# Rotary attention with a SoLU MoE layer on one core: a new order of issue, new second engines and new buffers for the same instructions

## Chip, core and metric

The kernel runs on one core of a Trainium2 chip. The core has five engines that run side by side, each with a queue of its own in program order: PE multiplies matrices, DVE and ACT work on tiles elementwise, POOL (GpSimd) does the same more slowly, and SP only issues DMA transfers. The metric is the time of one execution on the device in microseconds (us), the median of several runs; lower is better.

## The reference

Attention with rotary position embedding on 4 batches of 8 heads (576 positions, 64 values each), then a layer on the 2304 tokens of 512 values that come out of it:

```python
q_rot, k_rot = (rotate(q), rotate(k))
scores = scale * np.matmul(q_rot, k_rot.transpose(0, 1, 3, 2))
scores = scores - np.max(scores, axis=-1, keepdims=True)
attn = np.exp(scores)
attn = attn / (np.sum(attn, axis=-1, keepdims=True) + 1e-09)
return np.matmul(attn, v).astype(np.float32)
...
h = x @ w_in
h_max = np.max(h, axis=-1, keepdims=True)
e = np.exp(h - h_max)
sm = e / (np.sum(e, axis=-1, keepdims=True) + 1e-09)
solu = h * sm
mu = np.mean(solu, axis=-1, keepdims=True)
var = np.mean((solu - mu) ** 2, axis=-1, keepdims=True)
ln = (solu - mu) / np.sqrt(var + 1e-06) * g_ln
return (ln @ w_out).astype(np.float32)
```

All is float32. `w_in` is 512x1024 and `w_out` 1024x512; both arrive as float64 bit patterns.

## The kernel before

**Tiles and stages.** Two heads make a pair, P0 to P15, four pairs to a batch; `attention(P)` (line 389) does one. A pair has nine score tiles of 128 rows by 576 columns: four row blocks times two heads, and a packed one for the 64 rows left over of each head. Each goes through the same steps: scores on PE (L421, L450 to L453, L444), the row maximum on DVE (L401, L464), the exponential on ACT (L403, L467), a transpose, and the product with V on PE (`av`, L556), which is done in two ranges of query columns. "A15.1" is the second range of the last pair. DVE scales that product into `xT` (L561). The transpose is done on PE with a copy out of PSUM (`tr`, L481, copies by L324 on ACT or L326 on DVE), or, from pair 4 on for 7 or 8 of the 8 full tiles, by a round trip of the exponentials through DRAM (`escr`) and a 32x32 block transpose on DVE (L502).

**Rope.** `rope` (line 357) turns q and k of a pair ahead of its attention: two products with the tables of cosine and sine and a sum, each 128x576, by `tt` (line 351, all at L355). From pair 4 on, q and k are split in a rounded high part (a cast, L324 or L326) and a low part (a subtraction, L355), and each score is the sum of three products.

**The layer.** When the four pairs of a batch are done, their tokens go in 18 tiles of 128 through `front` (line 606: x split in high and low part, 24 matmuls L626, maximum L633, exponential L635, product L637, a DRAM round trip) and `back` (line 662: block transposes L681, high and low part L686 and L691, 24 matmuls L699, scaling L702 and L704, the store). `weights` (line 748) turns the float64 weights into high and low parts beside the first pairs' attention: for each of 16 pieces a load, a step on ACT (L777), four on DVE (L779, L781, L783, L785), a cast and a subtraction. `norm` (line 565) turns the sums of exponentials into reciprocals (L570, L571) and spreads them by DRAM (`rscr`, `Rb`).

**What sets the order.** All these functions only write down steps: `add` (line 203) keeps for each of 2365 steps its engine, its function and what it reads and writes. The steps are then issued in the order of the list `ORDER` (line 31), so each engine's queue is that list, cut down to its own steps; the semaphores that steps of different engines need follow from what they read and write. A step with `alt=` has a second engine that can do it as well (products, sums and subtractions by `tt`: DVE or POOL; casts and copies: ACT or DVE), and it goes there where its number stands in `FLIP` (line 161). A step of a rope runs on POOL unless flipped, a product of the prologue on DVE. `BUFS` (line 168) has a digit for each of 401 uses of a buffer, out of three score buffers of two PSUM banks ("D", `pd`), two of one bank ("G", `pg`) and three in SBUF ("B", `tb`). All three tables were written by a planner outside this file. The loop that issues:

```python
    for us, b in zip(pl.uses, BUFS):
        us[2] = int(b)
    engines = {"act": nc.scalar, "dve": nc.vector, "pool": nc.gpsimd}
    with tc.manual_schedule():
        for i in ORDER:
            if i in pl.alts:
                a = pl.alts[i]
                pl.ops[i][3](engines[a[2] if i in FLIP else a[0]])
            else:
                pl.ops[i][3]()
```

**The first steps.** `prologue` (line 709) loads the tables (steps 5 and 6), k (8 for the first half of its features, 9 and 10 for the second in two pieces) and q (7 for 192 columns, 11 for the rest), and ropes pair 0 in pieces: q's first 192 columns by steps 16, 17 and 18, its other 384 by 24, 25 and 26, k by 19 (576 columns), 20 and 21 (288), 22 and 23 (288). The first scores need 18, 21 and 23.

Of the kernel before, what the change touches and what calls it, by code (L numbers as in the profile page):

```python
# [31 lines left out]
    2, 3, 4, 5, 8, 6, 10, 7, 9, 11, 27, 35, 19, 12, 22, 23, 17, 20, 21, 16, 91, 18, 43, 25, 102, 24, 26, 28,  # L32
    105, 92, 99, 103, 106, 13, 29, 36, 111, 30, 31, 104, 37, 109, 114, 107, 93, 110, 112, 115, 32, 113, 135,
    38, 108, 51, 39, 33, 116, 122, 123, 138, 97, 124, 117, 136, 125, 139, 118, 126, 40, 120, 119, 144, 137,
    94, 59, 121, 96, 95, 44, 155, 128, 41, 145, 127, 142, 147, 129, 45, 42, 148, 100, 130, 156, 14, 143,
    131, 98, 132, 157, 1, 133, 146, 151, 134, 101, 46, 186, 152, 163, 164, 47, 52, 0, 165, 153, 177, 187,
    166, 167, 154, 140, 189, 188, 158, 48, 141, 195, 159, 178, 168, 190, 169, 53, 179, 160, 67, 149, 196,
    161, 162, 170, 193, 198, 197, 181, 184, 150, 219, 194, 34, 199, 180, 191, 206, 171, 182, 207, 192, 222,
    172, 68, 220, 173, 54, 221, 174, 55, 175, 223, 69, 202, 183, 70, 60, 185, 176, 228, 203, 56, 49, 50,
    208, 200, 229, 209, 210, 239, 201, 231, 230, 71, 224, 232, 72, 226, 225, 61, 212, 270, 73, 62, 211, 63,  # L40
    227, 75, 74, 437, 204, 240, 235, 205, 271, 241, 213, 265, 273, 214, 236, 215, 272, 509, 264, 216, 217,
    274, 275, 266, 279, 276, 64, 269, 57, 218, 83, 76, 58, 244, 237, 282, 245, 246, 238, 277, 280, 283, 233,
    261, 281, 303, 247, 278, 248, 77, 234, 78, 249, 350, 306, 250, 251, 284, 304, 307, 242, 262, 312, 243,
    351, 305, 253, 252, 263, 84, 288, 254, 323, 285, 290, 268, 79, 65, 80, 289, 66, 255, 313, 256, 473, 257,
    291, 314, 315, 258, 352, 324, 316, 259, 15, 292, 260, 293, 325, 85, 294, 317, 86, 267, 438, 308, 87,
    357, 362, 309, 331, 358, 345, 81, 295, 296, 318, 82, 332, 286, 363, 328, 287, 330, 329, 88, 364, 346,
    326, 365, 333, 353, 446, 371, 361, 327, 334, 439, 335, 366, 347, 310, 372, 321, 311, 374, 297, 440, 375,
    360, 298, 441, 299, 373, 354, 300, 322, 301, 447, 382, 442, 395, 474, 448, 455, 666, 302, 337, 380, 398,
    336, 369, 381, 396, 319, 370, 449, 397, 367, 450, 399, 404, 451, 368, 660, 464, 89, 415, 661, 320, 90,
    348, 383, 405, 384, 376, 385, 475, 386, 378, 377, 349, 338, 406, 416, 339, 407, 379, 340, 341, 662, 408,  # L50
    409, 476, 465, 675, 477, 342, 417, 388, 343, 387, 665, 355, 456, 677, 359, 478, 410, 667, 344, 479, 482,
    389, 678, 390, 452, 391, 680, 679, 356, 676, 392, 466, 393, 681, 423, 467, 400, 457, 685, 688, 394, 401,
    682, 424, 761, 512, 425, 413, 513, 689, 426, 427, 414, 411, 691, 690, 402, 468, 714, 692, 469, 480, 696,
    765, 518, 403, 481, 686, 470, 519, 715, 717, 520, 683, 693, 483, 458, 521, 459, 412, 418, 718, 701, 514,
    702, 460, 716, 722, 515, 484, 697, 668, 485, 725, 429, 486, 419, 663, 487, 703, 516, 704, 664, 471, 726,
    705, 420, 517, 672, 694, 422, 728, 727, 430, 431, 684, 766, 723, 531, 432, 491, 421, 433, 488, 730, 687,
    434, 489, 532, 719, 435, 729, 522, 737, 674, 767, 707, 695, 523, 537, 428, 706, 538, 490, 738, 461, 699,
    524, 533, 768, 669, 700, 539, 492, 731, 724, 735, 770, 772, 534, 443, 527, 720, 493, 535, 739, 494, 495,
    540, 444, 740, 496, 445, 536, 736, 698, 500, 777, 497, 525, 498, 436, 708, 472, 778, 550, 709, 732, 710,
    779, 551, 711, 453, 712, 782, 746, 526, 776, 741, 499, 713, 556, 747, 721, 742, 557, 528, 501, 673, 748,  # L60
    552, 749, 502, 670, 750, 733, 503, 553, 783, 504, 734, 743, 462, 505, 554, 463, 780, 506, 588, 555, 752,
    541, 781, 754, 751, 454, 755, 507, 785, 744, 745, 542, 756, 753, 508, 867, 757, 758, 543, 558, 774, 784,
    559, 545, 544, 760, 510, 592, 786, 569, 762, 560, 593, 594, 775, 589, 606, 788, 511, 590, 759, 561, 591,
    791, 789, 570, 792, 595, 562, 790, 596, 796, 671, 529, 793, 814, 801, 530, 563, 802, 769, 866, 803, 597,
    804, 817, 603, 805, 598, 815, 818, 797, 599, 607, 771, 816, 825, 763, 819, 610, 608, 794, 764, 838, 826,
    624, 600, 822, 828, 827, 609, 601, 839, 829, 602, 868, 820, 862, 878, 833, 604, 869, 798, 799, 611, 605,
    613, 830, 840, 612, 614, 795, 564, 615, 546, 881, 823, 547, 616, 841, 861, 879, 617, 882, 628, 618, 800,
    863, 886, 787, 571, 806, 834, 836, 619, 565, 876, 821, 548, 837, 807, 864, 575, 831, 873, 847, 865, 880,
    824, 620, 883, 889, 625, 877, 549, 566, 621, 887, 808, 874, 848, 890, 809, 810, 892, 891, 811, 622, 893,
    576, 894, 962, 835, 629, 849, 915, 626, 850, 832, 851, 627, 812, 884, 577, 902, 623, 870, 578, 813, 903,  # L70
    916, 904, 572, 918, 917, 961, 842, 888, 573, 905, 920, 919, 854, 900, 773, 574, 871, 843, 897, 901, 872,
    963, 923, 926, 579, 895, 853, 844, 630, 927, 906, 580, 855, 852, 845, 856, 929, 928, 967, 857, 885, 898,
    858, 846, 930, 921, 859, 581, 966, 924, 936, 931, 938, 937, 896, 582, 968, 978, 875, 860, 939, 631, 973,
    899, 940, 632, 969, 633, 922, 941, 970, 634, 932, 981, 635, 908, 925, 982, 567, 636, 642, 568, 986, 979,
    989, 947, 980, 637, 990, 639, 983, 638, 933, 907, 971, 991, 909, 640, 964, 910, 994, 992, 1015, 977,
    965, 948, 993, 643, 942, 987, 974, 997, 911, 943, 1016, 912, 984, 644, 1018, 913, 1017, 645, 1000, 914,
    1002, 1001, 1020, 934, 949, 646, 1026, 935, 950, 951, 1003, 1252, 944, 1027, 995, 955, 946, 945, 956,
    1028, 1029, 1253, 957, 998, 988, 1030, 976, 1004, 958, 1019, 1254, 1005, 985, 959, 1006, 1023, 1037,
    1039, 952, 647, 1038, 583, 954, 996, 649, 648, 953, 1021, 1264, 1040, 1034, 584, 999, 1041, 650, 1007,
    1042, 651, 1265, 1008, 1247, 652, 1267, 1266, 1024, 653, 1248, 1031, 1268, 585, 1269, 654, 641, 960,  # L80
    1022, 1249, 1275, 1035, 1009, 1276, 586, 1010, 587, 1048, 1011, 1277, 1278, 1012, 1259, 1013, 1032,
    1025, 1301, 1263, 1280, 1014, 1279, 1270, 1062, 655, 1272, 1063, 657, 656, 1283, 1049, 1288, 1262, 1250,
    1050, 1064, 1051, 1251, 1052, 1068, 1033, 1065, 1069, 1036, 1353, 1043, 1302, 1070, 1281, 1044, 1304,
    1066, 1303, 1352, 658, 1071, 1305, 1271, 1045, 1273, 1255, 1067, 1047, 1256, 1284, 1312, 1081, 1072,
    1309, 1306, 1056, 972, 1315, 1073, 1054, 1057, 1053, 1313, 1348, 1058, 975, 1316, 1046, 1074, 1314,
    1324, 1354, 1289, 1317, 1286, 1325, 1055, 1059, 1082, 1359, 1287, 1060, 1326, 1282, 1310, 1364, 1327,
    1347, 1285, 1307, 1257, 1076, 1087, 1363, 1349, 1365, 1290, 1088, 1291, 1274, 1292, 1328, 1089, 1077,
    1329, 1318, 1367, 1090, 1366, 1075, 1333, 1334, 1322, 1061, 1368, 1083, 1311, 1323, 1375, 1355, 1308,
    1335, 1320, 1336, 1378, 1084, 1337, 1321, 1453, 1362, 1376, 1085, 1379, 1294, 1319, 1293, 1330, 1377,
    1086, 1078, 1357, 1260, 1157, 1401, 1100, 1091, 1338, 1332, 1331, 1101, 1350, 1339, 1295, 1402, 1340,  # L90
    1092, 1296, 1383, 1297, 1404, 1079, 1372, 1341, 1454, 1093, 1405, 1342, 1403, 1343, 1409, 1388, 1258,
# [818 lines left out]
```

## Time and profile before

| what | value |
|---|---|
| three runs, us | 448.65, 453.29, 454.40 |
| median of the runs, us | 453.29 |
| profiled execution, span from its first to its last instruction, us | 452.4 |
| TensorE's granted clock in it | 1.000 |
| instructions in it | 8070 |
| HBM read and written, MB | 70.91 and 37.82 |

The span is the profiled execution's own time as far as it is known: no other time is told for that execution, and what lies around its first and last instruction is in the runs' times alone. The median of the runs is 0.9 us above the span.

A time at an engine's instruction is from its start to its end as the profiler saw it. DVE's and POOL's instructions overlap their neighbours by up to 0.1 us. PE's matmuls are pipelined, so a matmul's record is longer than the time that it adds; the chain that ended last counts only what it adds.

### The profile page before, as it was taken

What the parts mean: (1) busy time and instruction counts of PE and PEld (TensorE: products, weight loads), DVE (VectorE), ACT (ScalarE), POOL (GpSimd) and SP (SyncE); (2) the same over time, 40 slices, a digit from 0 to 9 for tenths busy, and PEclk for the clock granted to TensorE, in tenths of its full rate; (3) what the DMA queues carried; (4) which work ended last, traced back from release to release, by engine and by line L of the source; (5) the groups of instructions that cost most, each with busy time, mean ns of one, the idle gap of its engine ahead of it and who ended that gap; (6) DMA issues with size and microseconds to landing.
All of it is one profiled execution on the core that took longest, in us unless ns stands there. A gap on an engine that the chain in (4) does not pass through costs nothing.

```text
span 452.4 us, 8070 instructions
## 1 busy us (share of the span) xinstructions
PE 427.1 (94%) x2676; PEld 309.4 (68%) x2676; DVE 395.7 (87%) x608; ACT 286.5 (63%) x653; POOL 223.8 (49%) x257
## 2 busy tenths in 40 slices
PE   1799888999999999999999999999999999999996
PEld 1466555677668666676677677668686777878885
DVE  3999999999999989999998899899799987877663
ACT  1698877999767557657757655767557664443422
POOL 0252524438789773746776947457461621112121
PEclk9999999999999999999999999999999999999999
DMA  8655646588899989999899998899999987533441
GB/s 259 251 170 190 204 146 220 184 250 249 264 291 283 299 255 285 296 309 287 269 292 325 279 308 276 256 284 276 291 297 264 275 250 243 172 133 130 163 140 47
DMA packets 92378, 109.28 MB, mean 242 GB/s; under 512 B 7456, under 2 KB 67888, under 8 KB 92336
## 3 DMA queue, kind: packets, MB, share of 16 engines
q1 hardware_dynamic: 92336, 108.76, 77.3%
q8 instruction: 21, 0.34, 0.4%
q14 instruction: 21, 0.17, 0.1%
HBM read 70.91 MB, written 37.82 MB: 240 GB/s over the span
## 4 chain that ended last, share of the span: by engine, by line
PE 64%; DMA 15%; DVE 11%; issue 4%; SPq 3%; ACT 3%; DVEq 0%; ACTq 0%
PE pd L626 18%; PE pg L699 16%; PE pg L556 12%; PE pd L421 8%; PE pg L481 6%; DMA e<-escr 5%; DMA escr<-e 4%; DVE mx L401 3%; SPq L339 3%; DMA uscr<-u 2%; DVE ET L502 2%; PE pd L444 2%; DMA rawq<-in_q_t_dram 2%; DMA wraw<-uscr 1%; ACT e L403 1%
## 5 line engine op out<-in xcount | busy, mean ns | idle before, releaser
L403 ACT ACTIVATE e<-pd,mx 128x576 f32<-128x576 f32 x132 | 97.3, 741 | 38.5 <-DVE mx L401 30.8
L502 DVE STREAM_TRANSPOSE ET<-e 128x512 f32<-128x512 f32 x90 | 99.7, 1131 | 3.7 <-DMA e<-escr 3.1
L401 DVE TENSOR_REDUCE mx<-pd 128x1 f32<-128x576 f32 x132 | 94.0, 743 | 6.4 <-PE pd L421 5.9
L556 PE MATMUL pg<-ET,vst 128*64 128x320 f32 (+1 forms) x512 | 69.8, 412 | 0.8 <-ACT ET L324 0.5
L626 PE MATMUL pd<-wih,xh 128*128 128x512 f32 x144 | 61.1, 424 | 0.2 <-ACT e L467 0.2
L481 PE MATMUL pg<-idn,e 128*128 128x128 f32 (+1 forms) x308 | 55.2, 297 | 4.7 <-DVE xT L561 1.6
L699 PE MATMUL pg<-woh,lnh 128*128 128x512 f32 x144 | 59.1, 410 | 0.0
L691 POOL TENSOR_TENSOR lnl<-tb,lnh 128x512 fp32r<-128x512 f32 x27 | 35.3, 1311 | 45.4 <-ACT lnh L324 34.9
L481 PEld LDWEIGHTS pg<-idn,e 128*128 128x128 f32 (+1 forms) x308 | 41.6, 186 | 22.7 <-issue 4.2
L699 PE MATMUL pg<-woh,lnl 128*128 128x512 f32 x144 | 56.5, 392 | 0.2 <-POOL lnl L691 0.2
L626 PE MATMUL pd<-wih,xl 128*128 128x512 f32 x144 | 56.6, 393 | 0.0
L699 PE MATMUL pg<-wol,lnh 128*128 128x512 f32 x144 | 56.2, 390 | 0.0
L626 PE MATMUL pd<-wil,xh 128*128 128x512 f32 x144 | 56.2, 390 | 0.0
L556 PEld LDWEIGHTS pg<-ET,vst 128*64 128x64 f32 x512 | 34.4, 136 | 25.0 <-issue 3.3
L681 DVE STREAM_TRANSPOSE tb<-wraw 128x512 f32<-128x512 f32 x36 | 38.7, 1097 | 3.3 <-DMA wraw<-uscr 2.7
L355 POOL TENSOR_TENSOR rawk<-rawk,tabs 128x576 f32<-128x576 f32 x21 | 31.0, 1476 | 21.1 <-DMA rawk<-in_k_t_dram 18.5
L324 ACT COPY ET<-pg 128x512 f32<-128x512 f32 x52 | 30.1, 587 | 17.3 <-PE pg L481 17.1
L355 POOL TENSOR_TENSOR rawq<-rawq,tabs 128x576 f32<-128x576 f32 x20 | 29.4, 1478 | 21.2 <-DMA rawq<-in_q_t_dram 19.3
L421 PE MATMUL pd<-kh,qh 64*128 64x288 f32 x192 | 34.6, 343 | 1.4 <-ACT e L403 1.3
L421 PE MATMUL pd<-rotk,rotq 64*128 64x288 f32 x128 | 23.7, 473 | 12.8 <-DVE rotq L355 9.3
L421 PEld LDWEIGHTS pd<-kh,qh 64*128 64x128 f32 x192 | 19.1, 184 | 19.5 <-issue 8.4
L626 PEld LDWEIGHTS pd<-wih,xh 128*128 128x128 f32 x144 | 27.3, 189 | 6.9 <-issue 2.1
(116 smaller groups left out, 878.4 us busy)
## 6 DMA issues: line engine op xcount, KB each, us to landing
escr<-e SPq DMA_DIRECT2D x90, 256.0 KB
e<-escr SPq DMA_DIRECT2D x90, 256.0 KB
uscr<-u SPq DMA_DIRECT2D x18, 512.0 KB
wraw<-uscr SPq DMA_DIRECT2D x18, 512.0 KB
rawk<-in_k_t_dram SPq DMA_DIRECT2D x15, 576.0 KB
rawq<-in_q_t_dram SPq DMA_DIRECT2D x15, 576.0 KB
vst<-in_v_t_dram SPq DMA_DIRECT2D x16, 320.0 KB
out_dram<-o SPq DMA_DIRECT2D x18, 256.0 KB
```

The costliest lines, as they stand in the source:

```text
L324: nc.scalar.copy(o, i)
L355: add(*c[0], prio, lambda e: e.tensor_tensor(o, a, b, op=op), r, w, alt=c[1], two=True)
L401: add("dve", 672, t, lambda: nc.vector.tensor_reduce(mx[:, mcol:mcol + 1], buf(us)[:, :, 0:288], axis=AX.XY, op=ALU.max, negate=True), [sk ...
L403: add("act", 720, t, lambda: nc.scalar.activation(e.rearrange("p (z n) -> p z n", z=2), buf(us)[:, :, 0:288], AF.Exp, bias=mx[:, mcol:mcol ...
L421: nc.tensor.matmul(buf(us)[:, z, 0:288], a[rows, c0:c0 + 128], w[rows, 288 * z:288 * z + 288], start=(j == 0), stop=(j == len(terms) - 1))
L481: nc.tensor.transpose(dst, src, idn)
L502: add("dve", 1040, t, lambda: nc.vector.transpose(ET[r][:, h, :, q0:q0 + 128].rearrange("p m (a j) -> p j m a", j=4), e.rearrange("p (j b ...
L556: nc.tensor.matmul(buf(uy)[rows, 0:nq], vv[:, m, h, :], e, start=(m == 0), stop=(m == 4))
L626: nc.tensor.matmul(buf(uh)[:, z, :], a[:, c, :], w[:, c, HF * z:HF * z + HF], start=(c == 0 and j == 0), stop=(c == KC - 1 and j == 2))
L681: add("dve", 1050, tl, lambda z=z, turned=turned: nc.vector.transpose(turned().rearrange("p m (a j) -> p j m a", j=4), v[:, :, 128 * z:128 ...
L691: add(*c[0], tl, lambda e, hd=hd, ld=ld, turned=turned: e.tensor_tensor(ld, turned(), hd, op=ALU.subtract), [bk] + kl[0][z], kl[1][z], use ...
L699: nc.tensor.matmul(buf(uo), a[:, f, :], w[:, f, :], start=(f == 0 and j == 0), stop=(f == FC - 1 and j == 2))
```

## The change

The functions stay as they are; the three tables have new values.

- `ORDER`: the same 2365 numbers in another order. Cut down to one engine, and without the steps that change their engine, 148 of 663 steps on PE, 190 of 531 on DVE, 159 of 434 on ACT, 112 of 221 on POOL and 185 of 417 on SP would have to move to turn the one queue into the other. On PE the mean step stands 1.3 places from where it stood, on SP and DVE 2 places, on ACT 3, on POOL 4; the largest moves are of 16 places on PE and 14 on SP.
- `FLIP`: 99 steps change their engine: 30 from DVE to POOL, 14 from POOL to DVE, 29 from DVE to ACT, 26 from ACT to DVE. DVE then has 571 steps (590 before), POOL 251 (235), ACT 463 (460). Among the 30 are steps 17, 22, 23 and 26 of the prologue.
- `BUFS`: 246 of the 401 digits differ.
- SP's first loads come in the order 8, 10, 5, 6, 9, 7, 11 (before: 5, 8, 6, 10, 7, 9, 11). DVE's first products are 19, 20, 21, 16, 18, 24, 25 (before: 19, 22, 23, 17, 20, 21, 16, 18, 25, 24, 26), and POOL's 22, 23, 17, 26.
- Behind the last step of A15.1, PE has 68 steps in both lists: the second halves of tile 12, the fronts of tiles 15 to 17 and the second halves of 13 to 17.

```diff
--- before.py
+++ after.py
 ORDER = [
-    2, 3, 4, 5, 8, 6, 10, 7, 9, 11, 27, 35, 19, 12, 22, 23, 17, 20, 21, 16, 91, 18, 43, 25, 102, 24, 26, 28,
-    105, 92, 99, 103, 106, 13, 29, 36, 111, 30, 31, 104, 37, 109, 114, 107, 93, 110, 112, 115, 32, 113, 135,
-    38, 108, 51, 39, 33, 116, 122, 123, 138, 97, 124, 117, 136, 125, 139, 118, 126, 40, 120, 119, 144, 137,
-    94, 59, 121, 96, 95, 44, 155, 128, 41, 145, 127, 142, 147, 129, 45, 42, 148, 100, 130, 156, 14, 143,
-    131, 98, 132, 157, 1, 133, 146, 151, 134, 101, 46, 186, 152, 163, 164, 47, 52, 0, 165, 153, 177, 187,
...
+    8, 1, 509, 10, 5, 19, 6, 22, 23, 9, 20, 21, 7, 11, 27, 28, 17, 12, 16, 18, 102, 24, 25, 26, 105, 106,
+    109, 35, 36, 103, 29, 13, 91, 93, 30, 31, 104, 37, 111, 114, 110, 107, 112, 43, 32, 115, 135, 113, 38,
+    116, 122, 108, 39, 92, 123, 51, 124, 117, 125, 138, 139, 126, 128, 127, 97, 118, 119, 136, 137, 2, 44,
+    120, 40, 144, 41, 94, 95, 142, 96, 100, 143, 147, 148, 145, 146, 98, 155, 129, 156, 130, 121, 131, 132,
+    133, 151, 45, 46, 47, 157, 163, 186, 52, 152, 33, 164, 101, 134, 187, 165, 166, 153, 59, 154, 167, 189,
...
 ]
 FLIP = {
-    34, 94, 96, 98, 178, 180, 181, 261, 262, 263, 264, 266, 329, 330, 334, 345, 351, 354, 358, 508, 590,
-    647, 660, 661, 662, 665, 673, 744, 745, 761, 765, 769, 843, 845, 850, 868, 945, 1005, 1046, 1062, 1063,
-    1120, 1213, 1248, 1250, 1251, 1259, 1260, 1287, 1356, 1360, 1424, 1456, 1524, 1532, 1533, 1588, 1592,
-    1649, 1706, 1782, 1803, 1805, 1873, 1882, 1902, 1904, 1907, 1983, 2004, 2085, 2162, 2164, 2180, 2200,
-    2218, 2219, 2237, 2257, 2277, 2278, 2280, 2296, 2313, 2317, 2332, 2334, 2350, 2352,
+    17, 22, 23, 26, 34, 94, 96, 98, 178, 180, 181, 236, 261, 265, 285, 322, 346, 347, 350, 352, 499, 508,
+    590, 608, 627, 644, 647, 661, 662, 665, 666, 672, 761, 765, 770, 773, 804, 846, 871, 945, 946, 969,
+    1062, 1063, 1138, 1159, 1163, 1198, 1214, 1250, 1257, 1260, 1287, 1336, 1357, 1449, 1451, 1460, 1588,
+    1649, 1687, 1781, 1782, 1841, 1903, 1987, 2164, 2165, 2180, 2181, 2218, 2219, 2257, 2277, 2281, 2296,
+    2299, 2313, 2317, 2334, 2349, 2350,
 }
 BUFS = (
-    "0210211100001112111000010011002011111010121010100021001000111200101100201102011210101112000111020011"
-    "0122102221212012010011001010020210010110112000122001101102010001010001111020101102102120001021221101"
-    "2101101011100020012000021211010101020200020010000012002000102100011102120111200202011120220200020111"
-    "1001111001010010211111010101001011012101021120001220112111001211112101010000002210021101021110012112"
+    "0200211100101011210101101020001101010210011012101010001201110021112010000102100200111010111210101100"
+    "1021001000112100211200120111121201201000212001122011111002120001212111101102100012102011010200201221"
+    "0201201121101201201211101100101000211211012120200101001000200100000112120110020202011010201001201100"
+    "0212001020101202100001001010101102001000002201112020101000120210001202111101022010211201112102001121"
     "0"
 )
 
```

## Rows read from the trace of the kernel before

**Rows 1.** The page: busy time (parts 1 and 2), one group of matmuls (part 5)
```profile
PE 427.1 (94%) x2676; PEld 309.4 (68%) x2676; DVE 395.7 (87%) x608; ACT 286.5 (63%) x653; POOL 223.8 (49%) x257
...
GB/s 259 251 170 190 204 146 220 184 250 249 264 291 283 299 255 285 296 309 287 269 292 325 279 308 276 256 284 276 291 297 264 275 250 243 172 133 130 163 140 47
...
L626 PE MATMUL pd<-wih,xh 128*128 128x512 f32 x144 | 61.1, 424 | 0.2 <-ACT e L467 0.2
```
**Rows 2.** Busy us (count) of PE, PEld, DVE, ACT, POOL by stage; clock, DMA share
```profile
20.00:220.00 200.00, 191.29 (x1283) 132.10 (x1281) 190.64 (x310) 153.01 (x361) 115.11 (x110) 1.00 0.79 245
220.00:380.00 160.00, 158.94 (x1045) 117.47 (x1042) 144.63 (x212) 100.47 (x233) 90.75 (x108) 1.00 0.93 283
380.00:452.40 72.40, 68.72 (x327) 54.36 (x323) 48.06 (x69) 26.49 (x48) 14.39 (x32) 1.00 0.41 137
```
**Rows 3.** The chain that ended last, its end: start us, us, what
```profile
399.41 2.84 PE pg L556 x20
...
427.64 21.09 PE pg L699 x93
...
448.83 0.75 DVE o L704
```
**Rows 4.** Timeline, DVE and POOL at 15 and 221 us: start us, us, instruction
```profile
15.35 1.63 DVE L779 TENSOR_SCALAR xT<-xT 128x512 f32<-128x512 f32 x1
...
15.29 1.40 POOL L355 TENSOR_TENSOR rawk<-rawk,tabs 128x576 f32<-128x576 f32 x1 [14.09 <-DMA rawk<-in_k_t_dram]
...
220.97 3.00 DVE L570 TENSOR_SCALAR acc<-acc 128x4 f32<-128x4 f32 x1
...
221.16 2.79 POOL L355 TENSOR_TENSOR rawk<-rawk,tabs 128x576 f32<-128x576 f32 x2
```
**Rows 5.** DVE's groups by form: busy us, mean ns, idle before
```profile
L779 DVE TENSOR_SCALAR xT<-xT 128x512 f32<-128x512 f32 x12 | 7.6, 632 | 0.1
L355 DVE TENSOR_TENSOR rawq<-rawq,tabs 128x576 f32<-128x576 f32 x10 | 7.5, 746 | 0.0
L781 DVE TENSOR_SCALAR xT<-xT 128x512 uint32<-128x512 uint32 x12 | 7.4, 620 | 0.2
...
L570 DVE TENSOR_SCALAR acc<-acc 128x4 f32<-128x4 f32 x16 | 7.2, 453 | 0.9 <-ACT e L403 0.9
...
L783 DVE SCALAR_TENSOR_TENSOR xT<-u,xT 128x512 uint32<-128x512 uint32 x5 | 4.6, 913 | 0.1
...
L570 DVE TENSOR_SCALAR acc<-acc 128x5 f32<-128x5 f32 x16 | 3.2, 200 | 0.0
...
L783 DVE SCALAR_TENSOR_TENSOR o<-wraw,o 128x512 uint32<-128x512 uint32 x4 | 2.8, 691 | 0.1
...
L781 DVE TENSOR_SCALAR o<-o 128x512 uint32<-128x512 uint32 x4 | 1.7, 424 | 0.1
```
**Rows 6.** The page, part 5: a rope's product on POOL
```profile
L355 POOL TENSOR_TENSOR rawq<-rawq,tabs 128x576 f32<-128x576 f32 x20 | 29.4, 1478 | 21.2 <-DMA rawq<-in_q_t_dram 19.3
```
**Rows 7.** Timeline of the first 16 us: DVE's first steps and PE's first matmul
```profile
4.36 0.76 DVE L355 TENSOR_TENSOR rawk<-rawk,tabs 128x576 f32<-128x576 f32 x1 [4.36 <-DMA rawk<-in_k_t_dram]
...
6.55 0.46 DVE L355 TENSOR_TENSOR rawk<-rawk,tabs 128x288 f32<-128x288 f32 x1 [1.43 <-DMA rawk<-in_k_t_dram]
...
7.42 0.35 DVE L355 TENSOR_TENSOR rawq<-rawq,tabs 128x192 f32<-128x192 f32 x1
...
9.35 2.29 PE L421 MATMUL pd<-rotk,rotq 64*128 64x288 f32 x8 [9.35 <-DVE rotq L355]
```
**Rows 8.** SP's own waits: who for whom, us in total, times, longest
```profile
SPq L339 <- DMA escr<-e: 44.8, 35, 3.9
SPq L339 <- ACT e L403: 33.6, 29, 3.7
```
**Rows 9.** The engines' waits: who for whom, us in total, times, longest
```profile
PEld pd L421 <- ACT e L403: 11.6, 19, 3.4
...
DVE ET L502 <- DMA e<-escr: 3.1, 4, 1.2
```

246 rows, old and new, of the table ORDER are left out of this document.

## Prediction

> **What bounds the kernel now.** I read the page's first part, then the busy time by stage, then the chain that ended last, and only then single instructions. The totals [rows 1] show two engines nearly full: PE 94% and DVE 87% busy; ACT at 63% and POOL at 49% have room. The stages [rows 2] tell which of the two it is where. From 20 to 220 us DVE is busy for 190.64 of 200 us: here DVE sets the pace. PE's busy time looks full too, but a matmul's record is up to 424 ns long [rows 1] where one follows the other every 227 ns (21.09 us for 93 of them [rows 3]), so PE's figure overstates it. From 220 to 380 us DVE has some slack (144.63 of 160) and PE shows no gap. After 380 us DVE is down to 48.06 of 72.40.
>
> The end of the chain [rows 3] is the most useful view. The last attention matmuls (A15.1, line 556) end at 402.25 us; from there PE goes from matmul to matmul, and DVE takes up the last result at 448.83. In the order list 68 PE steps stand behind A15.1, of three matmuls each: 204 matmuls of 0.227 us make 46.3 us, and 402.25 + 46.3 = 448.6. So this tail is pure work, and the span can shrink only if A15.1 ends earlier. In the new list 68 PE steps stand behind A15.1 as well. The question is how much earlier A15.1 comes, and that is mainly a question of the DVE stage.
>
> There DVE hardly waits for data, but some of its instructions take far longer than their work. At 15.35 us a clamp of 128x512 (L779) takes 1.63 us; a POOL tensor_tensor ran from 15.29 for 1.40 us [rows 4]. At 220.97 an addition on 128x4 elements takes 3.00 us, beside two POOL instructions one right after the other (2.79 us). So a DVE instruction of this kind stands still until POOL is done, and all of DVE's queue stands behind it: the row maxima first, which ACT's exponentials and so PE's next scores wait for. How much this is in all, from the means by form [rows 5]: L779 12 x (632 - 424) ns = 2.5 us, with the 424 ns of the undisturbed L781 as the free price; L781 12 x (620 - 424) = 2.4; L783 5 x (913 - 691) = 1.1; L570 16 x (453 - 200) = 4.0. These 10.0 us I call the port loss.
>
> **The change part by part.** The instructions stay. What changes is who comes first in each queue, which engine executes some of them, and which buffer they use.
>
> *Second engines.* 99 choices differ. Those between DVE and ACT (29 copies go to ACT, 26 come) about cancel; those between DVE and POOL don't. Ahead of DVE's step of A15.1, 17 rope or low-part steps of 576 columns leave DVE for POOL and 8 come back: 9 x 0.746 = 6.7 us less [rows 5]. Four first steps leave DVE (0.46 + 0.46 + 0.35, and some 0.6 for 384 columns: 1.9 us) [rows 7]; three LayerNorm low parts of 512 columns come, at 512/576 of 0.746 each: 2.0 us. Net 6.6 us less on DVE. By stage, step for step: 1.9 ahead of 20 us, 0.9 from 20 to 220, 3.9 from 220 to 380. The 0.9 counts in full: -0.9. The 3.9 falls where PE shows no gap; I take a third, -1.3 (bounds 0 and -3.9).
>
> *The head.* PE begins at 9.35 us, when DVE has done seven steps back to back from 6.55 [rows 7]. Now POOL takes three of them (two of 288 columns, one of 192) and DVE keeps four. POOL's price is 1.478 us for 576 columns [rows 6], about double of DVE's 0.746. If both run side by side, PE starts at 6.55 + 0.74 + 0.74 + 0.49 + 0.35 (DVE's closing sum) = 8.9. If they exclude each other, DVE's four (1.62) and POOL's three (1.97) make 3.6 us, and PE starts at 10.1. So -0.5 to +0.8; I take +0.3, nearer to exclusion, which [rows 4] show for other pairs. The first cosine table is loaded third instead of first; the product that needs it, now at 4.36 us, may come as late as 6.55 at no cost.
>
> The Trainium skill ("SBUF — State Buffer", section "Who interferes with whom") says that DVE and GpSimd share one port pair under an exclusive lock, held for a whole instruction by whoever issues first, and that a DVE tensor_tensor with both inputs in SBUF falls under it against a GpSimd instruction that reads SBUF. The 1.63 us at 15.35 agrees for a clamp; no row of the head has both engines on tensor_tensor. By that rule the head alone would be +0.8 in place of +0.3, and the sum 0.5 us longer.
>
> *Order of issue.* A fifth of PE's steps, a third of DVE's and ACT's, half of POOL's and nearly half of SP's stand elsewhere relative to their neighbours, mostly by one to four places; the order of the stages is the same. The port loss can be planned away in part: it hangs on which 1.4 us instruction of POOL meets which 0.4 us instruction of DVE. Bounds 0 and -10.0; I take -6.0, a little over half, since much of it is few long meetings such as those in [rows 4]. New meetings: from 20 to 240 us 16 steps go from DVE to POOL and 11 come back, 5 more, each between 0 and one POOL instruction of 1.4 us (0 to +7). The nearest row is the average over what POOL does now, 10.0 us over some 150 long instructions (223.8 us of POOL at 1.478 each): 5 x 0.07 = +0.3. DVE's 9.4 us of idle time from 20 to 220 is the other thing that an order can fill: a sixth, -1.5 (bounds 0 and -9.4).
>
> *SP's queue and the buffers.* SP issues every DMA in order, and what waits at its front holds up the rest. Its largest waits are for the round trip of the exponentials through DRAM (44.8 us in 35) and for the exponentials themselves (33.6 us in 29) [rows 8]. What they would hurt is DVE's block transposes (L502), which wait only 3.1 us for their landings now [rows 9]. I cost the reordering of SP at nothing: DVE's own queue hides it. If that cover is gone, as it may be after 220 us, one wait at SP's front shows in DVE with its length, up to 3.9 us. Of the buffer choices 246 of 401 differ; a bad one shows as PE's weight load waiting for an exponential that still reads a scores buffer, 11.6 us in 19 waits now [rows 9]. Also nothing, between -2 and +2.
>
> **Sum.** Against the profiled execution: 452.4 + 0.3 - 0.9 - 6.0 + 0.3 - 1.5 - 1.3 = 443.3 us of span. The median of the three runs, 453.29, lies 0.9 above the profiled span, so 444.2 us as a median. The three runs lie between 448.65 and 454.40; 2% (9.1 us) is about what a measurement of this kernel can tell from no change.
>
> **The rivals.**
> *Much faster.* The whole port loss goes, DVE's idle time halves almost (-4), and the later stage follows fully: 452.4 - 0.9 - 10.0 - 4 - 3.9 + 0.9 = 434.5. For it: nothing but work stands behind A15.1, so what is gained ahead of it is kept, and POOL is free for 85 of 200 us [rows 2], so there is room to keep the two apart. Against: a meeting is decided by 0.4 us, and the runs shown differ by 5.8.
> *No change: the transfers are the bound.* From 220 to 380 us the DMA engines are busy to 93% and move 283 GB/s [rows 2]. If that is their limit, an earlier DVE finds data that is not there, A15.1 comes as before, and only part of the first stage's gain is left: 450 to 453. Against: a slice of the page reaches 325 GB/s [rows 1], and DVE's transposes wait 3.1 us in all.
> *Slower: POOL in the way.* POOL's extra steps stand back to back, as at 221.16, DVE waits behind pairs of them, and a rope that POOL ends later (1.478 instead of 0.746) holds up the next pair's scores on PE, which issues in order. Place: the ropes of pairs 3 to 7, between 45 and 150 us. Price: if meetings double, +10.0, and for five steps of 0.73 us more on the way to the scores +3.7: 453.3 - 0.9 + 13.7 = 466. It decides once the port loss of the new profile is above some 20 us (10.0 now, 0.9 saved, 9.1 for 2%).
> *The plan doesn't hold on the chip.* The order is made for landings that the chip may not have; then waits move and the sum stays: 448 to 457. Nothing in the profile excludes it; the 5.8 us between three runs speak for it.
>
> **How the numbers follow.** The forecast's case (438 to 449) has 0.55, half of it under 444.2; much faster (428 to 438) 0.17; the two cases of no change (449 to 460) 0.19; slower 0.09. Faster by over 2%: 0.28 + 0.17, with rounding 0.46; slower 0.09; within 2% the rest, 0.45. The range leaves out half of much faster and most of slower: 434 to 456.
>
> **What would show it.** Right: A15.1's matmuls end near 393 us, with 46 us of matmuls without a gap behind them; the means of L779, L781 and L570 fall towards 424 and 200 ns; DVE's busy time falls by some 14 us and POOL's grows by some 18. Wrong: means of L779 and L570 as before or higher (the port was not planned around); DVE waiting over 10 us for its landings (SP or the transfers); PE starting after 10 us (the head); PE waiting longer for exponentials (the buffers). The prediction falls as a whole if A15.1 ends earlier and the span doesn't follow, or if it ends after 400.

## The result, and the profile after

The changed kernel takes 456.34 us as a median of 19 runs (452.24 to 460.33), the kernel before beside it 451.66 (19 runs, 448.36 to 455.96). The ratio is 1.010, 95% interval 1.007 to 1.013: 1% slower. The forecast was 444.2, 2% faster, with a range up to 456.0, so the time lies 0.3 us above the range. By the 2% bound the two count as the same, which had 0.45.

In the runs whose span is known the time is about 1.8 us above the span (the prediction took 0.9). So the profiled execution of the kernel before (span 452.4) stands for about 454.2 us, one of its longer runs, and that of the changed kernel (451.5) for 453.3, one of its shorter. The two profiles can't be subtracted to get the 1%. What they show is where time went.

The page's first part and the stages of the changed kernel, to be held against [rows 1, 2]:

```profile
PE 428.4 (95%) x2676; PEld 311.7 (69%) x2676; DVE 387.9 (86%) x589; ACT 285.4 (63%) x656; POOL 241.5 (53%) x273
```

```profile
20.00:220.00 200.00, 192.17 (x1262) 133.05 (x1259) 188.40 (x302) 147.58 (x350) 120.52 (x114) 1.00 0.79 247
220.00:380.00 160.00, 160.00 (x1071) 119.81 (x1071) 144.95 (x211) 104.52 (x246) 94.75 (x112) 1.00 0.91 285
380.00:451.50 71.50, 67.78 (x321) 53.51 (x315) 43.90 (x61) 26.72 (x49) 19.34 (x36) 0.99 0.40 131
```

POOL has 17.7 us more work, as forecast (some 18). DVE has 7.8 us less (some 14 forecast). From 20 to 220 us DVE's busy time falls by 2.2 us and PE's rises by 0.9: little of what DVE saved reached PE. From 220 to 380 us PE has no gap at all; before, it had 1.06 us without a matmul there [rows 2].

The end of the chain, the lines that answer to [rows 3]:

```profile
398.47 2.84 PE pg L556 x20
...
426.02 21.77 PE pg L699 x96
```

A15.1 ends at 398.47 + 2.84 = 401.3 us (402.25 before, about 393 forecast), and the span ends 50.2 us later, as before (452.4 - 402.25). That part of the forecast holds: behind A15.1 is only work. Ahead of it this pair of profiles shows 0.9 us won, where some 9 were forecast.

DVE's groups by form (busy us, mean ns, idle before), to be held against [rows 5]:

```profile
L781 DVE TENSOR_SCALAR xT<-xT 128x512 uint32<-128x512 uint32 x12 | 6.8, 563 | 0.2
...
L570 DVE TENSOR_SCALAR acc<-acc 128x4 f32<-128x4 f32 x16 | 6.0, 376 | 0.3 <-ACT e L403 0.3
L779 DVE TENSOR_SCALAR xT<-xT 128x512 f32<-128x512 f32 x12 | 4.9, 414 | 0.0
...
L783 DVE SCALAR_TENSOR_TENSOR xT<-u,xT 128x512 uint32<-128x512 uint32 x5 | 3.6, 713 | 0.1
...
L783 DVE SCALAR_TENSOR_TENSOR xT<-wraw,xT 128x512 uint32<-128x512 uint32 x3 | 3.3, 1087 | 0.1
```

The four groups from which the forecast took its port loss have lost more than half of it: L779 12 x (414 - 424), L781 12 x (563 - 424), L783 5 x (713 - 691) and L570 16 x (376 - 200) ns are together 4.5 us, where they were 10.0. But other forms now stand beside POOL: the three L783 on `wraw` take 1087 ns where they took 692. The line of before:

```profile
L783 DVE SCALAR_TENSOR_TENSOR xT<-wraw,xT 128x512 uint32<-128x512 uint32 x3 | 2.1, 692 | 0.1
```

A measure of all such delays: take DVE's products, sums, additions and casts that don't touch PSUM, by line and shape, and add up what each takes over the tenth percentile of its group. This excess is 16.3 us before and 14.2 after. The planned meetings went; others came.

The head, from the timeline (start us, us, instruction), to be held against [rows 7]:

```profile
6.57 0.79 POOL L355 TENSOR_TENSOR rawk<-rawk,tabs 128x288 f32<-128x288 f32 x1 [5.65 <-DMA tabs<-in_tab_dram]
6.90 0.77 DVE L355 TENSOR_TENSOR rawk<-rawk,tabs 128x288 f32<-128x288 f32 x1 [0.58 <-DMA rawk<-in_k_t_dram]
7.44 0.88 POOL L355 TENSOR_TENSOR rotk<-rawk 128x288 f32<-128x288 f32 x1
7.71 0.93 DVE L355 TENSOR_TENSOR rotk<-rawk 128x288 f32<-128x288 f32 x1
...
9.81 0.85 PE L421 MATMUL pd<-rotk,rotq 64*128 64x288 f32 x2 [9.81 <-DVE rotq L355]
```

DVE's product of 288 columns takes 0.77 and its sum 0.93 us, where each took 0.46 alone; POOL's take 0.79 and 0.88, where half of [rows 6] is 0.74. The two engines seem to take turns. PE starts at 9.81 in place of 9.35: +0.46, near the +0.3 of the forecast. DVE's first product of 288 columns begins at 6.90 in place of 6.55, behind the landing of k, so up to 0.35 of the 0.46 may be a later start and not the sharing. The exclusive lock that the Trainium skill describes ("SBUF — State Buffer", "Who interferes with whom") agrees with these rows for two tensor_tensors too, though not the +0.8 that the prediction worked out for full exclusion.

SP's queue, the waits that answer to [rows 8]:

```profile
SPq L339 <- ACT e L403: 43.9, 37, 3.5
SPq L339 <- ACT rs L324: 41.4, 23, 3.6
...
SPq L339 <- DMA escr<-e: 11.0, 15, 2.1
```

SP's waits moved from the round trips (44.8 to 11.0 us) to the exponentials (33.6 to 43.9) and the sums (30.9 to 41.4), and DVE's waits no longer show one for the round trip of the exponentials (3.1 us in [rows 9]). In this profile that cost nothing, as assumed.

### The profile page after: what moved, and what is told of

It reads as the page before. It is cut to its first block, busy times and chain, and to the rows that moved or that the text cites. A ratio compares the mean times of both kernels' runs of the same rounds, so it can differ in the third digit from the quotient of the medians.

```text
span 451.5 us, 8054 instructions
## 1 busy us (share of the span) xinstructions
PE 428.4 (95%) x2676; PEld 311.7 (69%) x2676; DVE 387.9 (86%) x589; ACT 285.4 (63%) x656; POOL 241.5 (53%) x273
## 4 chain that ended last, share of the span: by engine, by line
PE 84%; DVE 7%; ACT 3%; DMA 3%; issue 2%; SPq 1%; DVEq 0%; ACTq 0%
PE pg L699 21%; PE pd L626 21%; PE pg L556 15%; PE pd L421 14%; PE pg L481 8%; PE pd L444 2%; DMA rawk<-in_k_t_dram 2%; DVE mx L401 2%; ACT e L403 2%; PE pg L573 1%; PE pg L805 1%; PE pd L450 1%; DVE acc L570 1%; DVE ET L502 1%; DMA e<-escr 1%
## 5 line engine op out<-in xcount | busy, mean ns | idle before, releaser
L401 DVE TENSOR_REDUCE mx<-pd 128x1 f32<-128x576 f32 x132 | 95.7, 746 | 14.3 <-PE pd L421 13.5
L556 PE MATMUL pg<-ET,vst 128*64 128x256 f32 (+1 forms) x512 | 69.5, 412 | 0.8 <-DVE EL L326 0.6
L481 PE MATMUL pg<-idn,e 128*128 128x128 f32 (+1 forms) x308 | 56.3, 301 | 5.1 <-ACT e L403 2.4
L626 PE MATMUL pd<-wih,xh 128*128 128x512 f32 x144 | 59.7, 415 | 0.0
L355 POOL TENSOR_TENSOR rawk<-rawk,tabs 128x576 f32<-128x576 f32 (+1 forms) x24 | 34.8, 1453 | 10.6 <-DMA tabs<-in_tab_dram 5.6
L421 PE MATMUL pd<-rotk,rotq 64*128 64x288 f32 x128 | 25.0, 502 | 11.2 <-DVE rotq L355 9.8
L421 PE MATMUL pd<-kh,qh 64*128 64x288 f32 x192 | 34.0, 343 | 0.5 <-ACT e L403 0.5
L355 POOL TENSOR_TENSOR rawq<-rawq,tabs 128x576 f32<-128x576 f32 (+1 forms) x22 | 30.7, 1398 | 4.4 <-DVE o L704 2.2
L699 PEld LDWEIGHTS pg<-woh,lnh 128*128 128x128 f32 x144 | 27.1, 188 | 6.9 <-issue 2.0
```

Of the source, the lines that this page charges most:

```text
L355: add(*c[0], prio, lambda e: e.tensor_tensor(o, a, b, op=op), r, w, alt=c[1], two=True)
L401: add("dve", 672, t, lambda: nc.vector.tensor_reduce(mx[:, mcol:mcol + 1], buf(us)[:, :, 0:288], axis=AX.XY, op=ALU.max, negate=True), [sk ...
L421: nc.tensor.matmul(buf(us)[:, z, 0:288], a[rows, c0:c0 + 128], w[rows, 288 * z:288 * z + 288], start=(j == 0), stop=(j == len(terms) - 1))
L481: nc.tensor.transpose(dst, src, idn)
L556: nc.tensor.matmul(buf(uy)[rows, 0:nq], vv[:, m, h, :], e, start=(m == 0), stop=(m == 4))
L626: nc.tensor.matmul(buf(uh)[:, z, :], a[:, c, :], w[:, c, HF * z:HF * z + HF], start=(c == 0 and j == 0), stop=(c == KC - 1 and j == 2))
```

## The experiments

The tables of the two kernels are called BEFORE and AFTER in the diffs. Unless it says otherwise, a step keeps its own kernel's engine and buffer; up to two buffer uses at a seam got another digit.

**The changed kernel again**, for a second profile, with no edit.

> The changed kernel once more, for a second profile and an interval of its own. Both theories: 1.007 to 1.013 of the kernel before. If its profiled span is near 455 us and not 451.5, the first profile was one of its quicker executions, and the loss can be looked for in this one.

Ratio 1.008 (1.005 to 1.011), span 452.9. This profile has a stretch that the first one hasn't. DVE, POOL, ACT and PE around it, from their timelines:

```profile
302.16 4.04 DVE L355 TENSOR_TENSOR rawq<-rawq,tabs 128x576 f32<-128x576 f32 x1
306.12 0.74 DVE L401 TENSOR_REDUCE mx<-pd 128x1 f32<-128x576 f32 x1
```

```profile
301.41 1.41 POOL L355 TENSOR_TENSOR ql<-rotq,qh 128x576 fp32r<-128x576 f32 x1
302.79 1.27 POOL L355 TENSOR_TENSOR xl<-xT,xh 128x512 fp32r<-128x512 f32 x1
304.02 0.18 POOL L660 TENSOR_TENSOR ms<-ms 128x1 f32<-128x1 f32 x1
304.16 1.42 POOL L355 TENSOR_TENSOR rawk<-rawk,tabs 128x576 f32<-128x576 f32 x1
```

```profile
306.96 0.74 ACT L403 ACTIVATE e<-pd,mx 128x576 f32<-128x576 f32 x1 [4.37 <-DVE mx L401]
```

```profile
310.28 0.40 PE L421 MATMUL pd<-kh,qh 64*128 64x288 f32 x1 [2.04 <-ACT e L467]
```

Step 1903, a product of q14's rope, went from POOL to DVE with the change. Here POOL runs from one instruction straight into the next, and DVE's stands until the row has ended: 4.04 us. In the first profile it took 0.75 us: it came 0.08 us ahead of POOL's next, and POOL's took 1.96 us in place of 1.41 (DVE, then POOL):

```profile
304.86 0.75 DVE L355 TENSOR_TENSOR rawq<-rawq,tabs 128x576 f32<-128x576 f32 x1
```

```profile
304.94 1.96 POOL L355 TENSOR_TENSOR ql<-rotq,qh 128x576 fp32r<-128x576 f32 x1
```

In the second profile a row maximum stands behind it on DVE, ACT waits 4.37 us for that, and PE 2.04 for ACT. Then, from the windows (PE busy comes first, the granted clock stands behind POOL):

```profile
308.00:311.80 3.80, 1.76 (x15) 1.34 (x16) 3.56 (x7) 3.20 (x8) 1.61 (x3) 1.00 0.55 202
311.80:315.20 3.40, 3.40 (x11) 2.57 (x10) 3.40 (x6) 1.90 (x5) 0.19 (x1) 0.50 0.96 287
```

PE was busy for 1.76 of 3.80 us, and the next 3.4 us were granted 0.50, the lower level of 1.2 GHz: half of them is lost as well. So this one stall of DVE costs PE 2.0 us of gap and some 1.7 us of slow matmuls.

**Only the engines, or only the order.**

```diff
 ORDER = BEFORE
-FLIP = BEFORE
+FLIP = AFTER
```

> Order and buffers of before, second engines of the change. Theory A (the new second engines cost: POOL's steps take twice DVE's time, and its port excludes DVE): 1.005 to 1.015. Theory B (the order of issue costs, the engines help since DVE has 6.6 us less to do): 0.99 to 1.00.

Ratio 1.036 (1.031 to 1.041).

```diff
-ORDER, BUFS = BEFORE
+ORDER, BUFS = AFTER
 FLIP = BEFORE
```

> Order and buffers of the change, second engines of before. Theory A: 0.99 to 1.002, the order alone is no loss. Theory B: 1.01 to 1.02, the order alone is the loss and DVE's saved work is missing too.

Ratio 1.072 (1.064 to 1.079). The busy times from 20 to 220 us, first engines alone, then order alone:

```profile
20.00:220.00 200.00, 185.57 (x1214) 126.34 (x1213) 182.73 (x292) 143.27 (x337) 117.64 (x108) 0.98 0.76 232
```

```profile
20.00:220.00 200.00, 183.96 (x1182) 126.21 (x1182) 178.31 (x290) 142.39 (x331) 110.33 (x103) 0.97 0.74 232
```

Both theories missed in both runs. Each half alone is much worse than both together, so the three tables belong together, and the 1% is no sum of an engine part and an order part. In both, DVE is busy for less than the 190.64 us of [rows 2] and so is PE: a kernel gets slower here while DVE has more time to spare, and part of it is the clock (0.98 and 0.97).

**Only the early or the late part** (EARLY: the first 743 steps of the old list, up to pair 6's first scores at 139 us).

```diff
-ORDER = BEFORE
+ORDER = [i for i in AFTER if i in EARLY] + [i for i in BEFORE if i not in EARLY]
```

> The change (order, engines, buffers) for the 743 steps that before issues ahead of pair 6's first scores (some 139 us), before's tables for the rest. If the loss is made in the first third (head, weights, ropes on POOL): 1.005 to 1.013, pair 6's scores 2 to 5 us later than before's 139.3. If it is made later: within 0.3% of before.

Ratio 1.015 (1.010 to 1.021).

```diff
-ORDER = AFTER
+ORDER = [i for i in BEFORE if i in EARLY] + [i for i in AFTER if i not in EARLY]
```

> The counterpart of early_after: before's tables for the 743 steps ahead of pair 6's first scores, the change for the rest. If parts add (1.0079 to 1.0101 for the whole, 1.0154 for the early part): 0.992 to 0.995, a kernel quicker than both. If the early part's 1.0154 is only a bad seam between two orders: 1.00 to 1.015, since this one has the same seam.

Ratio 0.996 (0.993 to 0.998). The two add up to the change: the early tables lose, the late ones win.

**The early part in three** (cut at pair 2's and pair 4's first scores, 45 and 86 us).

```diff
-ORDER = BEFORE
+ORDER = BEFORE[:a] + [i for i in AFTER if i in BEFORE[a:b]] + BEFORE[b:]
```

with a and b 0 and 198, 198 and 428, 428 and 743.

> The change for the first 198 steps alone (to pair 2's first scores, some 45 us), before's tables for the rest. Theory head (POOL's prologue products and DVE's exclude each other): PE starts 0.5 us later, 1.001 to 1.004. Theory weights (the loss is made from 45 to 139 us, where DVE is full with weights and ropes): 0.998 to 1.002.

> The change for the 230 steps between pair 2's and pair 4's first scores alone (45 to 86 us). Theory weights: 1.005 to 1.012, with pair 4's first scores 2 to 5 us later than 86.3. Theory head: 0.995 to 1.002.

> The change for the 315 steps between pair 4's and pair 6's first scores alone (86 to 139 us). Theory weights: 1.003 to 1.01. Theory head: 0.997 to 1.002. A shift that this part makes should stay to the end unchanged, as it did from 185 us on in early_after (4.8 us at pair 8, 3.9 at pair 15).

Ratios 1.007 (1.003 to 1.010), 1.003 (1.000 to 1.005) and 1.013 (1.009 to 1.016). The largest part of the early loss comes with the third segment. Together the three lose more than the early part as a whole (0.7 + 0.3 + 1.3 against 1.5 per cent), so the seams between two orders cost something too. The first came out above the range of the head theory, the second below that of the weights theory and the third above it.

**The third segment with one cast moved.** In this kernel an old order of ACT's steps meets new engines of a rope. In its profile ACT waited 2.58 us, up to 139.94 us, with a cast of q7 at the front of its queue.

```diff
-    878, 833, 604, 869, 798, 799, ...
+    878, 833, 604, 798, 799, ...
-    811, 622, 893, 576, 894, 962, ...
+    811, 622, 893, 869, 576, 894, 962, ...
```

> The kernel with the changed tables between pair 4's and pair 6's first scores only (ratio 1.0126), but with q7's cast on ACT (step 869) behind the exponentials of S6.1, where the change has it. Theory: the 4.5 us of PE's idle time at 137 to 150 us come from that cast, which stood at the front of ACT's queue and waited for POOL's rope while exponentials stood behind it; then these gaps fall to about 1.5 us and the ratio to 1.002 to 1.006. Rival: DVE's meetings with POOL's added rope steps are the cause; then PE's gaps stay at some 4 us and the ratio at 1.010 to 1.015.

Ratio 1.012 (1.008 to 1.016): the theory fell. ACT's wait went, and PE's gaps stayed. Its PE and POOL timelines:

```profile
144.64 0.50 PE L699 MATMUL pg<-woh,lnl 128*128 128x512 f32 x1 [1.50 <-POOL lnl L691]
...
150.17 0.40 PE L421 MATMUL pd<-kh,qh 64*128 64x288 f32 x2 [1.36 <-ACT e L403]
```

```profile
139.00 1.43 POOL L355 TENSOR_TENSOR rotq<-rawq 128x576 f32<-128x576 f32 x1
140.38 1.30 POOL L355 TENSOR_TENSOR xl<-xT,xh 128x512 fp32r<-128x512 f32 x1
141.63 1.44 POOL L355 TENSOR_TENSOR rawk<-rawk,tabs 128x576 f32<-128x576 f32 x1
143.01 0.33 POOL L355 TENSOR_TENSOR qzl<-rotq,qzh 64x64 fp32r<-64x64 f32 x1
143.29 1.29 POOL L691 TENSOR_TENSOR lnl<-tb,lnh 128x512 fp32r<-128x512 f32 x1
```

For the first gap PE waits for a low part that is last in an unbroken row on POOL. Ahead of the second another cast (`kh`) stands at the front of ACT's queue and waits 1.15 us for POOL's sum. This is the rival of the prediction, "POOL in the way", in its place (45 to 150 us), though at a few us and not at 13.7. It belongs to this mixed kernel: the profiles of the changed kernel have neither gap, so its 1.3% can't be carried over to the change.

**Less and more work on DVE.** The clamp of the 16 weight pieces (L779) is left out, or executed twice; both otherwise are the kernel before.

```diff
-lambda t=t: nc.vector.tensor_scalar(t, t, EXP_LO, EXP_HI, op0=ALU.max, op1=ALU.min)
+lambda: None
```

> The kernel before without the clamp of the weight pieces (L779, 16 instructions on DVE between 14 and 150 us; what is left out is only that clamp): 9.6 us of DVE's busy time by the rows of before, 6.8 us at its undisturbed 424 ns. Theory A (my prediction's: DVE sets the pace from 20 to 220 us): A15.1 and the end come 6.8 to 9.6 us earlier, ratio 0.979 to 0.985. Theory B (the end follows PE's idle time, of which the kernel before has no more than some 8 us between 20 and 220; DVE's work counts only where PE stands and waits for it): 0 to 3 us earlier, ratio 0.993 to 1.000.

```diff
-lambda t=t: nc.vector.tensor_scalar(t, t, EXP_LO, EXP_HI, op0=ALU.max, op1=ALU.min)
+lambda t=t: [nc.vector.tensor_scalar(t, t, EXP_LO, EXP_HI, op0=ALU.max, op1=ALU.min) for _ in range(2)]
```

> The kernel before with each of these 16 clamps executed twice: at least 6.8 us more on DVE. Theory A: at least 6.8 us later, ratio 1.015 or more. Theory B: DVE was busy for 190.6 of 200 us and some of its added work must reach PE, but less than its length: ratio 1.002 to 1.012; PE's idle time grows by as much as the span does.

Without the clamp the ratio is 0.994 (0.992 to 0.997): 2.6 us won by 11.7 us less on DVE (384.0 against 395.7). With it twice the ratio is 1.032 (1.028 to 1.036): 14.2 us lost by 13.0 more. Neither theory had both. The windows, first less, then more:

```profile
20.00:220.00 200.00, 195.08 (x1318) 134.88 (x1318) 184.88 (x299) 154.94 (x366) 117.49 (x112) 1.00 0.81 252
```

```profile
20.00:220.00 200.00, 184.43 (x1199) 124.99 (x1200) 189.77 (x306) 142.63 (x334) 111.09 (x101) 0.98 0.74 230
```

Taking work from DVE brings PE from 191.3 to 195.1 of 200 us, which leaves 4.9 us without a matmul. Adding work leaves DVE as full as it was, and PE falls to 184.4, with some stretches at the lower clock. The kernel before stands at the corner where both engines are nearly full.

**Two meetings taken apart in the changed kernel.** In both its profiles pair 6's normalisation stood beside two products of POOL, and PE waited. DVE, POOL and PE of the first:

```profile
152.23 2.78 DVE L570 TENSOR_SCALAR acc<-acc 128x4 f32<-128x4 f32 x1
```

```profile
152.20 2.79 POOL L355 TENSOR_TENSOR rawq<-rawq,tabs 128x576 f32<-128x576 f32 x2
```

```profile
155.28 0.27 PE L573 MATMUL pg<-idn,acc 128*4 128x128 f32 x1 [1.15 <-DVE acc L571]
```

The experiment puts two DVE steps behind it, and step 1903 back on POOL.

```diff
-    892, 893, 821, 834, 886, 897, 890, 621, 620, 622, 808, ... 854, 902, 903, 894, ...
+    892, 893, 834, 886, 897, 890, 821, 621, 620, 808, ... 854, 902, 903, 622, 894, ...
-    1649, 1687, 1781, 1782, 1841, 1903, 1987, ...
+    1649, 1687, 1781, 1782, 1841, 1987, ...
```

> The changed kernel with two meetings at DVE and POOL taken apart: pair 6's first normalisation (its L570 stood 2.78 us beside two products of POOL in both profiles, and PE waited 1.15 us for it) comes earlier on DVE, by a row maximum put ahead of a block transpose and the output scaling L704 put behind it; and the rope product of q14 (step 1903, 4.04 us in one profile, 0.75 in the other) goes back to POOL. Theory C (such meetings give back what the change wins): PE's wait at L573 in pair 6 goes, no gap at 300 to 310 us, ratio 1.000 to 1.006 in place of 1.010. Rival D (what is lost is lost in the first 86 us and these two cost nothing at the end): 1.008 to 1.012.

Ratio 1.003 (1.000 to 1.006). But PE's wait at pair 6 was still there, 1.77 us in place of 1.15, so the gain can hardly have come from it:

```profile
149.68 2.62 DVE L570 TENSOR_SCALAR acc<-acc 128x4 f32<-128x4 f32 x1 [0.95 <-ACT e L403]
```

```profile
149.49 2.78 POOL L355 TENSOR_TENSOR rawq<-rawq,tabs 128x576 f32<-128x576 f32 x2
```

L570 waits for the exponential now, and POOL's pair starts 0.2 us ahead of it again.

**Step 1903 alone, and then with cover for PE.**

```diff
 FLIP = AFTER
-    1649, 1687, 1781, 1782, 1841, 1903, 1987, ...
+    1649, 1687, 1781, 1782, 1841, 1987, ...
```

> The changed kernel with one engine choice undone: the rope product of q14 (step 1903) on POOL as before. Theory C1 (this one product stood up to 4.04 us behind POOL's row of products, the row maxima behind it, and so gave back most of what the change lost): as the kernel with both meetings taken apart, ratio 1.001 to 1.005, and no stretch of PE at half clock after 300 us. Rival (the two moves on DVE did it): 1.008 to 1.012.

Ratio 1.004 (1.001 to 1.008), no gap of PE after 220 us.

```diff
-    811, 812, 915, 904, 625, 576, 577, 626, ...
+    811, 812, 915, 576, 577, 904, 625, 626, ...
```

> As the run beside it, and two matmul groups of the layer (steps 576 and 577) ahead of pair 6's transposition of its sums on PE, as before: that transposition waited 1.13 to 1.77 us for a reciprocal that DVE could not start beside POOL. Theory: the wait has cover again and PE's gap at 150 to 156 us goes; A15.1 ends 1 us earlier, ratio 0.998 to 1.003. Rival (what is gained there is lost at the next wait): as the run beside it.

Ratio 1.004 (1.000 to 1.007). PE's wait for the reciprocal is gone from the profile, and PE waits 0.55 and 1.05 us at two later places (S6.3 and S8.3, for exponentials; 0.67 at the second of them in the run beside it). The two readings can't be told apart by the times.

**The better hybrid, with step 1903 on POOL.**

```diff
 ORDER = [i for i in BEFORE if i in EARLY] + [i for i in AFTER if i not in EARLY]
-    1460, 1588, 1649, 1687, 1781, 1782, 1841, 1903, 1987, ...
+    1460, 1588, 1649, 1687, 1781, 1782, 1841, 1987, ...
```

> The tables of before up to pair 6's scores and the changed ones behind them (ratio 0.9959), with step 1903 on POOL. In the profile of that kernel the product took 1.40 us on DVE in place of 0.75, so there is little to win: ratio 0.993 to 0.997. If the product on DVE was what the later part won by, 0.998 to 1.002.

Ratio 0.993 (0.990 to 0.997), 446.73 us beside 450.39: ahead of both kernels of the change. Its interval overlaps that of the late part alone (0.993 to 0.998), so what step 1903 adds there isn't shown.

**The kernel before again**, with no edit.

> The kernel before, once more, for a second profile. If the first profiled execution (span 452.4) was one of its slower ones, as the common first stretch of the other kernels says (3.3 us earlier at pair 4's scores), this span lies near 449, with pair 4's first scores at 83 us in place of 86.3.

Ratio 0.999 (0.995 to 1.003). The span is 450.7 and pair 4's scores come at 86.3 us, as in the first profile: the expectation missed. But of the other kernels with the same tables for the first 86 us, three have them at 83.0, 83.1 and 83.6 us (the late part, and the two of the third segment), and one at 85.8 (the late part with step 1903 on POOL). DVE and POOL in the two kinds of execution, first of this kernel:

```profile
45.98 1.80 DVE L783 SCALAR_TENSOR_TENSOR xT<-u,xT 128x512 uint32<-128x512 uint32 x1
...
55.39 1.51 DVE L781 TENSOR_SCALAR xT<-xT 128x512 uint32<-128x512 uint32 x1
```

```profile
45.96 1.28 POOL L355 TENSOR_TENSOR wil<-xT,wih 128x512 fp32r<-128x512 f32 x1 [2.09 <-ACT wih L324]
47.19 1.86 POOL L355 TENSOR_TENSOR rawq<-rawq,tabs 128x576 f32<-128x576 f32 x1
```

and of the kernel with the old tables up to pair 6, the same steps:

```profile
44.48 0.69 DVE L783 SCALAR_TENSOR_TENSOR xT<-u,xT 128x512 uint32<-128x512 uint32 x1
...
52.86 0.43 DVE L781 TENSOR_SCALAR xT<-xT 128x512 uint32<-128x512 uint32 x1
```

```profile
44.63 1.66 POOL L355 TENSOR_TENSOR wil<-xT,wih 128x512 fp32r<-128x512 f32 x1 [2.32 <-ACT wih L324]
```

With one list, POOL is 0.02 us ahead in the one execution and DVE waits 1.1 us; in the other DVE is 0.15 us ahead and POOL waits 0.4. Two such meetings make 2.2 us; the one execution was 1.5 us behind already when the first of them began (45.98 against 44.48), and at pair 4's scores it is 3.3 behind. Who comes first is not in the tables. By the times, this profile (452.43 us) is the longest of this kernel's 8 runs here and the first one was among the longer of its 19, so no profile shows a usual execution of the kernel before.

## Why the prediction was wrong

Two steps failed: DVE's saved time was counted one for one as time of the kernel, and the port loss was to fall by 6.0 us with only 0.3 of new meetings.

- *What bounds the kernel* was half right. "From 20 to 220 us DVE sets the pace" holds for added work (13.0 us cost 14.2) but not for saved work (11.7 us gave 2.6), and a gain was forecast. At that rate of 2.6 for 11.7 the forecast's 9.1 us would be some 2 (an estimate). The row that says it was there: PE busy for 191.29 of the same 200 us [rows 2]. I set it aside because matmul records overlap, but an overlapping record can make a short gap shorter, not a long one. PE had 8.7 us without a matmul from 20 to 220 us; the terms for that stretch (-0.9, -6.0, +0.3, -1.5) sum to -8.1, nearly all of it. The chain that ended last points the same way: DVE is 11% of it, PE 64% (part 4 of the page of the kernel before).

```profile
PE 64%; DMA 15%; DVE 11%; issue 4%; SPq 3%; ACT 3%; DVEq 0%; ACTq 0%
```

- *The port loss, -6.0, and new meetings, +0.3.* The four groups did lose 5.5 us. The new meetings, costed at an average of 0.07 us a step, were 3.4 us in the first profile (-2.1 in all, less the -5.5). In the second the four groups come to 3.7 us and the excess in all to 17.5: 17.5 - 16.3 + 6.3 = 7.5 us. So the two terms, -5.7 together, measured -2.1 and +1.2. My bounds for the new meetings were 0 and +7; the second profile is above the upper one. A mean over POOL's instructions was the wrong row: one meeting cost up to all that was left of POOL's unbroken row (DVE's product took 4.04 us in place of 0.75), and what stands behind it on DVE.
- *The port loss as a price* is itself in doubt. The excess over the tenth percentile doesn't order the kernels: it is 15.8 us in the second profile of the kernel before, but 13.6 with the third segment changed (ratio 1.013), 15.0 with the early part (1.015) and 16.9 with the order alone (1.072). What does follow the time is PE: in all 18 profiles it is busy for 424.5 to 437.1 us, while the spans go from 444.9 to 477.0 (at the upper end some 8.5 us of the busy time went to the lower clock). So nearly all of a difference in time is PE standing still or running at the lower clock, and a meeting seems to cost only what of it reaches PE.
- *Second engines*: the count was right (POOL +17.7), the value not: DVE's busy time from 220 to 380 us didn't fall (144.63 and 144.95), and PE had only 1.06 us without a matmul there, so the -1.3 had little to gain. One of these choices, step 1903, is what the runs show of the loss: with it on DVE the ratios are 1.010 and 1.008, in the three kernels with it back on POOL 1.003, 1.004 and 1.004. That is some 0.5% of the 1%. The stall of 4.04 us is the one way of it that was seen, in one of two profiles; how often it comes was not measured.
- *The head* (+0.3, measured +0.46, of which up to 0.35 is the later start that the sum didn't have), *the tail of pure work*, *SP at nothing* and *the buffers at nothing* (PE's weight load waits 5.4 us for exponentials at L421, 11.6 before) came out in size.
- *What would show it* named the case: "if it ends after 400" A15.1 falsifies the whole, and it ended at 401.3. Of the rivals, "the plan doesn't hold on the chip" (448 to 457) has the number, and "POOL in the way" the nearest mechanism, at a smaller price.

Open: the 0.3 to 0.4% that stay when step 1903 is undone. By the early and the late part they would come ahead of 139 us, if the seam between the two is no part of it. The head (0.46), the early meetings and PE's wait at pair 6 (1.15 us, at 154 us and so behind that border) are candidates that the runs didn't separate. Other stalls are left as well: a mean granted clock of 0.996 or less, which one stretch of 3.4 us at 0.50 makes, stands in 15 of the changed kernel's 31 runs, in 10 of the 36 with step 1903 on POOL and in 11 of the 111 of the kernel before.

## What to carry to other kernels

When two engines are both busy for 95% of a stretch, cap the gain from unloading one by the idle time of the other: read that number first. It is only a cap (8.7 us here, and 2.6 came). Here margins of 0.02 to 0.15 us decided which of two engines came first, and they changed from one execution to the next, so don't build a schedule on them; give DVE's step a place where POOL has a gap, or put PE work in front of whoever waits for it. Price a move to POOL by up to the unbroken row that it makes there, and ask what stands behind the DVE instruction that will meet it.

## What the runs showed of the hardware

- DVE's instruction can wait through several POOL instructions that follow each other without a gap: 4.04 us beside three long ones and a short one, and 2.78 beside two. The page of the Trainium skill named above tells of a lock for one instruction; in these rows the next POOL instruction takes it again. That is the rarer case. In the 18 profiles 136 of DVE's instructions were held up (by over 0.25 us) with a second long POOL instruction right behind the first; 15 waited through that too, 14 of them the addition of 128x4 (L570) and one step 1903. The others went on behind the first, as here in the first profile of the changed kernel (DVE, then POOL). What decides it stays open.

```profile
144.51 0.76 DVE L570 TENSOR_SCALAR acc<-acc 128x5 f32<-128x5 f32 x1
```

```profile
143.81 1.44 POOL L355 TENSOR_TENSOR rotq<-rawq 128x576 f32<-128x576 f32 x1
145.20 1.44 POOL L355 TENSOR_TENSOR rawk<-rawk,tabs 128x576 f32<-128x576 f32 x1
```

- An addition on 128x4 elements, 0.2 us of work, was held up for 2.78 us by two products of 576 columns on POOL.
- PE at 1.76 of 3.80 us busy was followed by 3.4 us at a granted clock of 0.50, so this gap of 2.0 us cost nearly twice its length.
